# Softmax of one batch written over its scores in PSUM, and its constant added one column at a time

## The chip, the cores and the metric

One core of a Trainium2 chip runs the kernel. The engines are named as the profile names them: PE (TensorE matmuls), PEld (its weight loads), DVE (VectorE), ACT (ScalarE), POOL (GpSimd) and SP (SyncE, which issues DMAs). The metric is the device time of one execution in microseconds (us), lower is better. The kernel before takes 1260.88 us (median of three runs, 1260.35 to 1262.1).

## The reference

Attention over blocks of 64 positions, then a feed-forward layer with a piecewise activation, all in fp32:

```
q, k, v: (8 batches, 8 heads, 576 positions, 64)
scores = q k^T / 8, and -1e9 where key block > query block (blocks of 64)
attn   = exp(scores - rowmax); attn = attn / (rowsum(attn) + 1e-9)
x      = (attn v), heads side by side: (4608, 512)
h      = x @ w_in            (512 x 2048)
g      = h where h >= 1; 0 where h <= -1; (h + 1)^2 / 4 between
out    = g @ w_out           (2048 x 512)
```

## The kernel before

The work goes by **pairs** of heads: 8 batches of 4 pairs. `attention_steps` walks the pairs in eight steps each and starts parts of the next pair (loading, splitting, turning q and k) between the softmax steps of the current one. For a pair, each head's 576 x 576 scores are made in row tiles of 128 queries against only the keys that are not masked: group 0 is two tiles side by side in one PSUM bank (128 and 256 columns), group 1 is one tile of 384, group 2 one of 512 columns. The last 64 queries of both heads of the pair share one more tile of 576 columns, in two banks (`scores_last`).

For each group, `scores` does this: PE makes the scores in a PSUM bank `ps` (L483, L486); DVE takes the negated row maximum `nm` of each tile (L506); ACT writes the exponential into the SBUF tile `pr`, and its row sum into one column of `sm` (L510); DVE adds the constant 1e-9 to all the sums of the group (L492 in `inverse`: a 128 x 2 operation for group 0, 128 x 1 for the others), takes the reciprocal (L493), and multiplies `pr` in place by it, tile by tile (L516). Then PE turns `pr` with an identity (`turn`, L553 or L555) and multiplies it with v (`weighted`, L592).

Batches differ in their treatment. Batch 0 turns `pr` directly. From batch 1 on (`HOP`) `pr` first goes through a DMA into another buffer. From batch 2 on (`FAR`, `RAW`, and no longer `PLAIN`) all operands are split into a high and a low word, and the work of a pair is spread further; `add_words` (L614, L615) then adds the two halves of the product with v.

**Banks.** PSUM has eight banks here: one for the feed-forward's `ph`, four in the pool `ps_o`, three in `ps_w`. `work_bank` hands them out in turn; up to the 36th step it alternates between `ps_o` and `ps_w`, after that `ps_o` belongs to the feed-forward's output and attention has the three of `ps_w`. A bank can be written again once everything that read it is done: for a score bank in the kernel before, that is the exponential.

**The rest of the work.** `prepare_weights` turns the weights into split words during the first two batches: ACT and DVE work on each piece (L169 to L177), then POOL (L183, L187), for which the pieces stand in three buffers. From step 36 one feed-forward step goes with each attention step: `ffn_in` (L771: 12 matmuls), the activation (ACT L780, DVE L781, DVE L784, ACT L785), POOL's `gl` (L786), and `ffn_out` of the piece before (L795, L800). When attention ends, the remaining feed-forward runs alone.

**Order.** The order of the instructions on each engine is fixed when the program is built, by the framework's scheduler: it follows the order in the text as a priority and lets work go ahead that is ready earlier. Each engine then takes its instructions strictly in that order, and each waits for its operands by semaphores. A change of one operation can therefore move others.

Of the kernel before, what the change touches and what calls it, by code (L numbers as in the profile page):

```python
# [10 lines left out]
AF = mybir.ActivationFunctionType  # L11
ALU = mybir.AluOpType
# [11 lines left out]
def block_attn_then_ffn(  # L24
# [9 lines left out]
    nc = tc.nc  # L34
# [19 lines left out]
    EPS = 1e-9  # L54
# [4 lines left out]
    HOP = 1  # L59
    FAR = 2  # L60
    RAW = 2

    const = ctx.enter_context(tc.tile_pool(name="const", bufs=1))
    att1 = ctx.enter_context(tc.tile_pool(name="att1", bufs=1))
# [12 lines left out]
    def work_bank(name):  # L77

        banks["n"] += 1
        if banks["free"] and banks["n"] % 2:  # L80
            return ps_o.tile([P, 512], F32, tag="po", name=name)
        return ps_w.tile([P, 512], F32, tag="work", name=name)
# [23 lines left out]
    def last_blocks(t_):  # L106
# [19 lines left out]
        out=msel[:NTL, : NTL * BLK].rearrange("p (t c) -> p t c", c=BLK),  # L126
# [106 lines left out]
    def as_float32r(src, plain):  # L233

        if plain:
            wide = src.shape[1] > RING - 2 * S
            places = SPARE_WIDE if wide else SPARE
            moved = [places[spare[wide] % len(places)]]
            spare[wide] += 1
            if src.shape[1] > TCH:  # L240
                if "end" not in spare:
                    spare["end"] = att1.tile([P, G0 + P], F32R, tag="pa11", name="pre")[:, :BLK]
                moved.append(spare["end"])
            for i, dst in enumerate(moved):
                n = min(TCH, src.shape[1] - i * TCH)
                nc.sync.dma_start(dst[:, :n].bitcast(F32), src[:, i * TCH : i * TCH + n])
            return moved
        n, moved = src.shape[1], []
        wide = wide_tile(F32R, "prr")
        nc.sync.dma_start(wide[:, :n].bitcast(F32), src)  # L250
        for c0 in range(0, n, TCH):
            moved.append(wide[:, c0 : min(c0 + TCH, n)])
        return moved


    class Pair:
# [4 lines left out]
        def __init__(self, b, hp):  # L261
# [6 lines left out]
            self.hop = b >= HOP  # L268
            self.raw = b >= RAW

# [218 lines left out]

        def inverse(self, total):  # L490

            nc.vector.tensor_scalar_add(total, total, EPS)  # L492
            nc.vector.reciprocal(total, total)  # L493

        def scores(self, j, g):
            tiles = self.GROUPS[g]
            m = len(tiles)
            ps = work_bank("ps_s")
            pr = att3.tile([P, S], F32, tag="pr", name="pr")
            nm = small.tile([P, 2], F32, tag="nm", name="nm")  # L500
            sm = small.tile([P, 2], F32, tag="sm", name="sm")
            cols = [slice(at, at + (t + 1) * P) for t, at in tiles]
            for (t, _), cs in zip(tiles, cols):
                self.product(ps[:, cs], j, t * P, 0, (t + 1) * P, True, True)
            for i, cs in enumerate(cols):
                nc.vector.tensor_reduce(  # L506
                    out=nm[:, i : i + 1], in_=ps[:, cs], axis=AX.X, op=ALU.max, negate=True
                )
            for i, cs in enumerate(cols):
                nc.scalar.activation(  # L510
                    pr[:, cs], ps[:, cs], AF.Exp, bias=nm[:, i : i + 1], scale=1.0,
                    accum_out=sm[:, i : i + 1],
                )
            self.inverse(sm[:, :m])
            for i, cs in enumerate(cols):
                nc.vector.tensor_scalar_mul(pr[:, cs], pr[:, cs], sm[:, i : i + 1])  # L516
            self.pr[j, g] = as_float32r(pr[:, : cols[-1].stop], self.plain) if self.hop else [pr]

        def scores_last(self):

            half = S // 2
            pr = att3.tile([P, S], F32, tag="pr", name="pr")
            nm = small.tile([P, 3], F32, tag="nm", name="nm")
            sm = small.tile([P, 3], F32, tag="sm", name="sm")
            banks = []
            for i in range(2):
                ps = work_bank("ps_s")
                for j in range(2):
                    self.product(ps[:, :half], j, SM, i * half, half, j == 0, j == 1)
                nc.vector.tensor_reduce(  # L530
                    out=nm[:, i : i + 1], in_=ps[:, :half], axis=AX.X, op=ALU.max, negate=True
                )
                banks.append(ps)
            nc.vector.tensor_tensor(out=nm[:, 2:3], in0=nm[:, 0:1], in1=nm[:, 1:2], op=ALU.min)
            for i in range(2):
                nc.scalar.activation(
                    pr[:, i * half : (i + 1) * half], banks[i][:, :half], AF.Exp,
                    bias=nm[:, 2:3], scale=1.0, accum_out=sm[:, i : i + 1],
                )
            nc.vector.tensor_tensor(out=sm[:, 2:3], in0=sm[:, 0:1], in1=sm[:, 1:2], op=ALU.add)  # L540
            self.inverse(sm[:, 2:3])
            nc.vector.tensor_scalar_mul(pr, pr, sm[:, 2:3])
            self.pr["last"] = as_float32r(pr, self.plain) if self.hop else [pr]

# [341 lines left out]
```

## Time and profile before

| what | value |
|---|---|
| runs | 1260.88, 1262.1, 1260.35 us |
| span of the profiled execution | 1262.2 us (1.3 us above the median run) |
| busy over the span | PE 1193.1 us (95%), DVE 888.1 (70%), ACT 695.3 (55%), POOL 375.3 (30%) |
| attention of batch 0 ends (last L516) | at about 106 us |
| attention of batch 1 ends (last L516) | at about 257 us |
| attention of the last batch ends (last L516) | at about 1065 us |
| granted TensorE clock, mean | 0.986: 0.90 up to 107 us, 0.95 from there to 257 us, 1.00 up to 1100 us |

All times are from one profiled execution, counted from the start of its span. A busy PE is not a PE at its peak, because matmuls overlap and their ends are modelled; idle time of PE, on the other hand, is time in which nothing ran on it. For what a wait costs, the row to read is the one that names the engine that waited and what released it.

### The profile page before, as it was taken

How to read it: one execution, taken by the hardware profiler on the slowest of the kernel's cores; microseconds unless marked ns; L12 is line 12 of the kernel's file. 1: busy time of each engine (PE TensorE's matmuls, PEld its weight loads, DVE VectorE, ACT ScalarE, POOL GpSimd, SP SyncE). 2: the span in 40 equal slices, each digit the busy share in tenths (PEclk: the TensorE clock that was granted, in tenths of full speed). 3: DMA queues.
4: the chain of work that ended last, by engine and by line, in shares of the span. 5: the costliest groups of instructions: out<-in, count | busy, mean ns of one | idle time of the engine just before them, and what ended most of it. 6: DMA issues, size and time to landing. Idle time of an engine off the chain costs nothing.

```text
span 1262.2 us, 19823 instructions
## 1 busy us (share of the span) xinstructions
PE 1193.1 (95%) x6280; PEld 995.7 (79%) x6280; DVE 888.1 (70%) x2092; ACT 695.3 (55%) x1731; POOL 375.3 (30%) x366
## 2 busy tenths in 40 slices
PE   4887988999999999999999999999999999999998
PEld 3665876788888888888888888888888888888886
DVE  8888688658777877787777877787778776222322
ACT  5776666446565666565556565565656655222222
POOL 3444556312222222222222222222222222222222
PEclk9887999999999999999999999999999999999999
DMA  5566676778887654565555545554556433422432
GB/s 162 167 183 208 215 253 213 217 219 236 277 270 242 187 151 146 163 195 158 148 151 174 179 144 156 153 179 140 161 156 188 143 118 119 133 93 91 134 101 100
DMA packets 177191, 215.39 MB, mean 171 GB/s; under 512 B 109872, under 2 KB 128304, under 8 KB 176320
## 3 DMA queue, kind: packets, MB, share of 16 engines
q1 hardware_dynamic: 177088, 214.14, 55.3%
q8 instruction: 50, 0.82, 0.3%
q14 instruction: 53, 0.43, 0.1%
HBM read 134.74 MB, written 31.98 MB: 132 GB/s over the span
## 4 chain that ended last, share of the span: by engine, by line
PE 69%; DVE 17%; ACT 5%; issue 5%; DMA 3%; POOL 1%; SPq 0%; ACTq 0%; DVEq 0%; POOLq 0%
PE ph L771 27%; PE po L795 15%; PE po L800 8%; PE ps_av L592 8%; PE ps_s L483 4%; PE ps_s L486 3%; ACT pr L510 3%; PE ps_t L553 2%; DVE pr L516 2%; DVE t L781 2%; DVE pb L548 2%; DVE t L784 2%; ACT t L780 2%; DVE nm L506 2%; DVE sm L492 1%
## 5 line engine op out<-in xcount | busy, mean ns | idle before, releaser
L786 POOL TENSOR_TENSOR gl<-t,gh 128x512 fp32r<-128x512 f32 x144 | 186.1, 1292 | 530.9 <-ACT gh L785 360.6
L795 PE MATMUL po<-wo,gh 128*128 128x512 f32 x1152 | 295.2, 397 | 0.1
L795 PEld LDWEIGHTS po<-wo,gh 128*128 128x128 f32 x1152 | 211.9, 189 | 43.6 <-ACT gh L785 0.6
L771 PE MATMUL ph<-xh,wih 128*128 128x512 f32 x576 | 231.4, 402 | 4.7 <-DVE t L784 4.4
L771 PE MATMUL ph<-xh,wil 128*128 128x512 f32 x576 | 226.8, 394 | 0.0
L771 PE MATMUL ph<-xl,wih 128*128 128x512 f32 x576 | 226.1, 393 | 0.0
L781 DVE SCALAR_TENSOR_TENSOR t<-t 128x512 f32<-128x512 f32 x144 | 101.8, 707 | 162.6 <-ACT t L780 159.6
L510 ACT ACTIVATE pr<-ps_s,nm 128x128 f32<-128x128 f32 (+3 forms) x256 | 133.9, 526 | 83.8 <-DVE nm L506 81.2
L780 ACT ACTIVATE t<-ph 128x512 f32<-128x512 f32 x144 | 85.9, 597 | 158.1 <-PE ph L771 158.1
L785 ACT CAST gh<-t 128x512 fp32r<-128x512 f32 x144 | 89.5, 621 | 121.0 <-DVE t L784 120.7
L800 PE MATMUL po<-wo,gl 128*128 128x512 f32 x576 | 155.4, 392 | 0.0
L483 PE MATMUL ps_s<-ka,qa 68*128 68x288 f32 (+4 forms) x384 | 134.7, 366 | 16.6 <-ACT pr L510 7.8
L506 DVE TENSOR_REDUCE nm<-ps_s 128x1 f32<-128x128 f32 (+3 forms) x256 | 119.0, 483 | 13.8 <-PE ps_s L486 12.9
L771 PEld LDWEIGHTS ph<-xh,wih 128*128 128x128 f32 x576 | 108.9, 189 | 24.2 <-DVE t L784 4.7
L771 PEld LDWEIGHTS ph<-xh,wil 128*128 128x128 f32 x576 | 108.8, 189 | 23.6
L800 PEld LDWEIGHTS po<-wo,gl 128*128 128x128 f32 x576 | 108.6, 189 | 22.9
L380 POOL TENSOR_TENSOR vsr<-vn,vsr 128x256 fp32r<-128x256 f32 (+1 forms) x96 | 56.4, 588 | 233.0 <-ACT vsr L379 232.0
L771 PEld LDWEIGHTS ph<-xl,wih 128*128 128x128 f32 x576 | 109.2, 190 | 19.3
L516 DVE TENSOR_SCALAR pr<-pr,sm 128x128 f32<-128x128 f32 (+3 forms) x256 | 118.4, 486 | 6.1 <-DMA ka<-kb 0.3
L486 PE MATMUL ps_s<-kb,qb 128*128 128x288 f32 (+4 forms) x384 | 120.9, 322 | 0.0
L492 DVE TENSOR_SCALAR sm<-sm 128x1 f32<-128x1 f32 (+1 forms) x224 | 55.8, 249 | 77.1 <-ACT pr L510 74.4
L784 DVE TENSOR_TENSOR t<-ph,t 128x512 f32<-128x512 f32 x144 | 98.7, 686 | 2.1
(111 smaller groups left out, 1811.9 us busy)
## 6 DMA issues: line engine op xcount, KB each, us to landing
wo<-wo_split SPq DMA_DIRECT2D x144, 512.0 KB, 3.4
prr<-pr SPq DMA_DIRECT2D x96, 192.0 KB, 2.5
prr<-pr SPq DMA_DIRECT2D x48, 256.0 KB, 2.6
out_dram<-ob SPq DMA_DIRECT2D x36, 256.0 KB, 2.3
bits<-in_moe_w_in_dram SPq DMA_DIRECT2D x16, 512.0 KB, 4.6
bits<-in_moe_w_out_dram SPq DMA_DIRECT2D x16, 512.0 KB, 4.0
wo_split<-ws SPq DMA_DIRECT2D x16, 512.0 KB, 3.0
qa<-qb SPq DMA_DIRECT2D x63, 128.0 KB, 2.4
```

Of the source, the lines that this page charges most:

```text
L483: nc.tensor.matmul(ps, qa[:KA, j, c0 : c0 + P], ka[:KA, j, k0 : k0 + n], start=first, stop=False)
L486: nc.tensor.matmul(ps, qb[:, j, c0 : c0 + P], kb[:, j, k0 : k0 + n], start=False, stop=last)
L506: nc.vector.tensor_reduce(out=nm[:, i : i + 1], in_=ps[:, cs], axis=AX.X, op=ALU.max, negate=True)
L510: nc.scalar.activation(pr[:, cs], ps[:, cs], AF.Exp, bias=nm[:, i : i + 1], scale=1.0, accum_out=sm[:, i : i + 1],)
L516: nc.vector.tensor_scalar_mul(pr[:, cs], pr[:, cs], sm[:, i : i + 1])
L771: nc.tensor.matmul(ph, w[:, cc, fs], x[:, cc, xs], start=(cc == 0 and i == 0), stop=(cc == NCC - 1 and i == 2),)
L780: nc.scalar.activation(t_, ph, AF.Relu, bias=0.5, scale=0.5)
L781: nc.vector.scalar_tensor_tensor(out=t_, in0=t_, scalar=1.0, in1=t_, op0=ALU.min, op1=ALU.mult)
L784: nc.vector.tensor_tensor(out=t_, in0=ph, in1=t_, op=ALU.max)
L786: nc.gpsimd.tensor_tensor(out=gl, in0=t_, in1=gh.bitcast(F32), op=ALU.subtract)
L795: nc.tensor.matmul(po[tt], gh[:, ts_], wo[:, w, :], start=(fc == 0 and w == 0), stop=False)
L800: nc.tensor.matmul(po[tt], gl[:, ts_], wo[:, 0, :], start=False, stop=fc == NFC - 1)
```

## The change

Three edits in `Pair`:

- In `scores`, for batch 0 alone (`AT_HOME = 1`), the exponential is written over the scores in their own PSUM bank, and the multiplication by the reciprocal reads that bank and writes `pr` in SBUF. Batches 1 to 7 keep `pr` for both.
- In `inverse`, the constant is added in one instruction per column: two of 128 x 1 for group 0, where there was one of 128 x 2. The reciprocal stays one instruction for the group.
- In `scores_last`, for all batches, the addition of the two half sums and the addition of the constant become one instruction with two operations, with the second half sum as a per-partition scalar.

```
+    AT_HOME = 1
...
         def inverse(self, total):
-            nc.vector.tensor_scalar_add(total, total, EPS)
+            for i in range(total.shape[1]):
+                nc.vector.tensor_scalar_add(total[:, i : i + 1], total[:, i : i + 1], EPS)
             nc.vector.reciprocal(total, total)
...
+            raw = ps if self.b < AT_HOME else pr
             for i, cs in enumerate(cols):
                 nc.scalar.activation(
-                    pr[:, cs], ps[:, cs], AF.Exp, bias=nm[:, i : i + 1], scale=1.0,
+                    raw[:, cs], ps[:, cs], AF.Exp, bias=nm[:, i : i + 1], scale=1.0,
                     accum_out=sm[:, i : i + 1],
                 )
             self.inverse(sm[:, :m])
             for i, cs in enumerate(cols):
-                nc.vector.tensor_scalar_mul(pr[:, cs], pr[:, cs], sm[:, i : i + 1])
+                nc.vector.tensor_scalar_mul(pr[:, cs], raw[:, cs], sm[:, i : i + 1])
...
-            nc.vector.tensor_tensor(out=sm[:, 2:3], in0=sm[:, 0:1], in1=sm[:, 1:2], op=ALU.add)
-            self.inverse(sm[:, 2:3])
+            nc.vector.tensor_scalar(
+                out=sm[:, 2:3], in0=sm[:, 0:1], scalar1=sm[:, 1:2], scalar2=EPS,
+                op0=ALU.add, op1=ALU.add,
+            )
+            nc.vector.reciprocal(sm[:, 2:3], sm[:, 2:3])
```

In the changed kernel the lines below the edits count a few higher: L492 becomes L494, L493 L495, L506 L508, L516 L519, L615 L621.

From batch 2 on, PE's order is the same, and that of the other engines nearly so but for the edits themselves. DVE, in such a batch at group 0 of a pair's first head (`sm` are its row sums; `x` is the pair before's sum of two halves, after which a bank is free for PE); before:

```order
L506 TENSOR_REDUCE nm<-ps_s 128x1 x2
L615 TENSOR_TENSOR x_5004<-ps_av,xtmp 64x256
L492 TENSOR_SCALAR sm<-sm 128x2
L493 RECIPROCAL sm<-sm 128x2
L615 TENSOR_TENSOR x_5004<-ps_av,xtmp 64x256
L516 TENSOR_SCALAR pr<-pr,sm 128x128
L516 TENSOR_SCALAR pr<-pr,sm 128x256
```

and now:

```order
L508 TENSOR_REDUCE nm<-ps_s 128x1 x2
L621 TENSOR_TENSOR x_5018<-ps_av,xtmp 64x256
L494 TENSOR_SCALAR sm<-sm 128x1 x2
L495 RECIPROCAL sm<-sm 128x2
L621 TENSOR_TENSOR x_5018<-ps_av,xtmp 64x256
L519 TENSOR_SCALAR pr<-pr,sm 128x128
L519 TENSOR_SCALAR pr<-pr,sm 128x256
```

One row has become two of one column each; nothing else has moved.

In batches 0 and 1 the scheduler has also moved other work. DVE, from the first group 0 of the first pair (`qa`, `ka` are q and k turned, `bits` and `shifted` the weights); before:

```order
L174 TENSOR_SCALAR shifted<-bits 128x512
L458 CAST qa<-ps_qk 64x2x64
L492 TENSOR_SCALAR sm<-sm 128x2
L177 SCALAR_TENSOR_TENSOR bits<-bits,shifted 128x512
L493 RECIPROCAL sm<-sm 128x2
L492 TENSOR_SCALAR sm<-sm 128x1
L458 CAST ka<-ps_qk 64x2x64
L516 TENSOR_SCALAR pr<-pr,sm 128x128
L516 TENSOR_SCALAR pr<-pr,sm 128x256
```

and now:

```order
L175 TENSOR_SCALAR shifted<-bits 128x512
L494 TENSOR_SCALAR sm<-sm 128x1
L459 CAST qa<-ps_qk 64x2x64
L494 TENSOR_SCALAR sm<-sm 128x1
L178 SCALAR_TENSOR_TENSOR bits<-bits,shifted 128x512
L495 RECIPROCAL sm<-sm 128x2
L494 TENSOR_SCALAR sm<-sm 128x1
L459 CAST ka<-ps_qk 64x2x64
L519 TENSOR_SCALAR pr<-ps_s,sm 128x128
L519 TENSOR_SCALAR pr<-ps_s,sm 128x256
```

The first column's addition now stands ahead of `qa`, and the multiplications read `ps_s`, the score bank, instead of `pr`. A few dozen rows further the two orders differ in where a weight piece's three DVE operations stand: before, one piece's operations were spread between the row maxima of the second pair, and now they stand together ahead of them.

## The prediction

> **What bounds the kernel now.** I read the stages first, one row each: the attention of batch 0 (up to 107 us), of batch 1 (up to 257 us), of batches 2 to 7 (up to 1100 us). Columns: the stretch, its length, then busy time and count of PE, PEld, DVE, ACT and POOL, granted clock, DMA share, GB/s.
>
> ```profile
> 0.00:107.00 107.00, 74.64 (x385) 60.21 (x385) 91.68 (x240) 72.50 (x187) 41.88 (x45) 0.90 0.60 176
> 107.00:257.00 150.00, 133.78 (x668) 106.98 (x668) 116.50 (x254) 94.87 (x226) 75.57 (x63) 0.95 0.71 222
> 257.00:1100.00 843.00, 827.69 (x4542) 699.35 (x4541) 638.14 (x1539) 491.12 (x1259) 220.45 (x229) 1.00 0.57 174
> ```
>
> In batch 0 DVE is busy 91.7 of 107 us and PE idles for 32.4. In the long stretch PE is busy 827.7 of 843 us: it is what the stage waits for, and only its 15.3 us of idle time can be won there. So the next view is PE's waits in the long stretch: who waited, for whom, us in total, times, the longest.
>
> ```profile
> PE ps_s L483 <- ACT pr L510: 7.8, 24, 0.4
> PE ps_qk L443 <- DVE x L615: 6.9, 19, 0.4
> ```
>
> These two make 14.7 of the 15.3 us, about once each in every one of the 24 pairs. Both come from work on DVE, so I looked for DVE operations that take longer than their size explains. The groups of the long stretch (line, engine, operation, shapes, count, then busy us and mean ns, then idle time before them):
>
> ```profile
> L492 DVE TENSOR_SCALAR sm<-sm 128x2 f32<-128x2 f32 x48 | 26.0, 542 | 26.0 <-ACT pr L510 26.0
> L492 DVE TENSOR_SCALAR sm<-sm 128x1 f32<-128x1 f32 x120 | 18.4, 153 | 41.0 <-ACT pr L510 38.6
> L516 DVE TENSOR_SCALAR pr<-pr,sm 128x384 f32<-128x384 f32 x48 | 20.1, 419 | 1.7 <-DMA ka<-kb 0.3
> L516 DVE TENSOR_SCALAR pr<-pr,sm 128x256 f32<-128x256 f32 x48 | 16.7, 348 | 0.0
> L516 DVE TENSOR_SCALAR pr<-pr,sm 128x128 f32<-128x128 f32 x48 | 13.8, 286 | 1.6
> ```
>
> The same addition takes 542 ns on two columns and 153 ns on one. One element more cannot cost 389 ns; something holds the instruction. The order of time shows what.
>
> **Term A: the first head's group 0, batches 2 to 7.** One pair; columns: start us, us, engine, line, operation.
>
> ```profile
> 502.88 1.29 POOL L786 TENSOR_TENSOR gl<-t,gh 128x512 fp32r<-128x512 f32 x1 [0.98 <-ACT gh L785]
> 503.03 0.19 ACT L510 ACTIVATION_READ_ACCUMULATOR pr<-ps_s,nm 128x1 f32 x1
> ...
> 503.70 0.37 ACT L614 COPY xtmp<-ps_av 64x256 f32<-64x256 f32 x1
> 503.71 0.49 DVE L492 TENSOR_SCALAR sm<-sm 128x2 f32<-128x2 f32 x1 [0.77 <-ACT pr L510]
> ...
> 504.23 0.17 DVE L493 RECIPROCAL sm<-sm 128x2 f32<-128x2 f32 x1
> ...
> 504.43 0.43 DVE L615 TENSOR_TENSOR x<-ps_av,xtmp 64x256 f32<-64x256 f32 x1
> ...
> 505.00 0.25 PE L443 MATMUL ps_qk<-ident_r,qk 128*128 128x128 f32 x1 [0.38 <-DVE x L615]
> ```
>
> The two-column addition starts at 503.71 and ends at 504.20, when POOL's gl ends (502.88 + 1.29 = 504.17). The reciprocal and x follow without a gap, and PE, which idled for 0.38 us, starts once x is done. So this is the wait on POOL, handed on to PE. The one-column form shows no such wait on average. In the changed kernel the first column's addition fits into the 0.77 us in which DVE idled, since its sum is there at 503.22; the second takes 0.15 us from 503.71. The reciprocal then ends near 504.07. Now x has another condition, ACT's copy, which ends at 503.70 + 0.37 = 504.07: x can start at 504.10 in place of 504.43. That is 0.33 us earlier, and PE has 0.38 us of idle time to give up. Over the 19 waits of the row: 19 x 0.33 = **6.3 us**. Bounds: nothing, if PE's next operand comes late anyway, and the row's 6.9.
>
> **Term B: the second head's group 0, same batches.**
>
> ```profile
> 519.95 1.29 POOL L786 TENSOR_TENSOR gl<-t,gh 128x512 fp32r<-128x512 f32 x1 [5.78 <-issue]
> ...
> 520.68 0.58 DVE L492 TENSOR_SCALAR sm<-sm 128x2 f32<-128x2 f32 x1 [0.27 <-ACT pr L510]
> ...
> 521.30 0.17 DVE L493 RECIPROCAL sm<-sm 128x2 f32<-128x2 f32 x1
> ...
> 521.50 0.55 DVE L516 TENSOR_SCALAR pr<-pr,sm 128x128 f32<-128x128 f32 x2
> ...
> 523.42 0.55 DVE L506 TENSOR_REDUCE nm<-ps_s 128x1 f32<-128x384 f32 x1
> ...
> 524.00 0.58 ACT L510 ACTIVATE pr<-ps_s,nm 128x384 f32<-128x384 f32 x1 [2.14 <-DVE nm L506]
> ...
> 524.72 0.50 PE L483 MATMUL ps_s<-ka,qa 68*128 68x512 f32 x1 [0.29 <-ACT pr L510]
> ```
>
> Again the addition ends with POOL's gl (519.95 + 1.29 = 521.24, against 521.26). From there DVE works without a pause up to the row maximum at 523.42, ACT's exponential waits for that, and PE waits 0.29 us for the exponential to free a bank. Here part of the gain is handed back: the addition would end at 520.83, the reciprocal at 521.03, and the multiplication, which works from SBUF to SBUF on many columns, stands before the same POOL operation until 521.24. It starts near 521.27 in place of 521.50: 0.23 us of the 0.43 remain. 24 x 0.23 = **5.5 us**; bounds nothing and the row's 7.8. A and B together: 11.8 us, between 0 and 14.7.
>
> **Term C: batch 0's multiplications.** All of them up to 107 us, the sum of the two halves in `scores_last`, and the row maxima, the nearest rows for an operation that reads one operand from PSUM:
>
> ```profile
> L516 DVE TENSOR_SCALAR pr<-pr,sm 128x384 f32<-128x384 f32 x8 | 7.7, 961 | 0.1
> L516 DVE TENSOR_SCALAR pr<-pr,sm 128x128 f32<-128x128 f32 x8 | 6.8, 850 | 0.0
> L516 DVE TENSOR_SCALAR pr<-pr,sm 128x256 f32<-128x256 f32 x8 | 6.2, 773 | 0.0
> L506 DVE TENSOR_REDUCE nm<-ps_s 128x1 f32<-128x512 f32 x8 | 5.5, 687 | 1.8 <-PE ps_s L486 1.7
> L506 DVE TENSOR_REDUCE nm<-ps_s 128x1 f32<-128x384 f32 x8 | 4.4, 548 | 0.0
> L516 DVE TENSOR_SCALAR pr<-pr,sm 128x512 f32<-128x512 f32 x8 | 3.9, 482 | 0.1
> L506 DVE TENSOR_REDUCE nm<-ps_s 128x1 f32<-128x256 f32 x8 | 3.3, 413 | 0.0
> ...
> L540 DVE TENSOR_TENSOR sm<-sm 128x1 f32<-128x1 f32 x4 | 2.4, 607 | 0.0
> L506 DVE TENSOR_REDUCE nm<-ps_s 128x1 f32<-128x128 f32 x8 | 2.3, 284 | 1.6 <-PE ps_s L486 1.6
> ```
>
> The multiplications take 7.7 + 6.8 + 6.2 + 3.9 = 24.6 us. Unhindered they would take 8 x (286 + 348 + 419 + 482 ns) = 12.3, by the long stretch's rows and this 512 row; the other 12.3 are waiting. One place shows on whom:
>
> ```profile
> 63.44 0.36 ACT L510 ACTIVATE pr<-ps_s,nm 128x128 f32<-128x128 f32 x1
> ...
> 65.62 1.40 POOL L365 TENSOR_TENSOR ks<-kn,ks 128x576 fp32r<-128x576 f32 x1 [0.25 <-DVE sm L493]
> 65.73 2.12 DVE L516 TENSOR_SCALAR pr<-pr,sm 128x128 f32<-128x128 f32 x2
> ...
> 66.97 0.66 POOL L315 MEMSET vs<- 128x320 f32 x2
> ...
> 68.48 0.42 DVE L171 TENSOR_SCALAR bits<-bits 128x512 f32<-128x512 f32 x1
> ```
>
> Two multiplications that need 0.63 us last 2.12, through POOL's ks (to 67.02) and its MEMSETs (to 67.63). Read from PSUM, I price them like the row maxima, which stay at one duration throughout: 8 x (284 + 413 + 548 + 687) = 15.5 us. So the price of reading PSUM is 3.2 us, the waits saved 12.3, net 9.1 on DVE. The fused sum saves another 4 x 607 = 2.4 us: the one instruction that stays costs what the L492 row shows for one column. Direct sum: 11.5 us.
>
> [...]
>
> How much of 11.5 is on the path? The chain of work that ended last, up to 107 us, by line:
>
> ```profile
> by line: DVE pr L516 12.0%; issue 11.3%; PE ps_av L592 11.0%; PE ps_t L555 6.6%; DVE nm L506 4.6%; DMA ka<-mrow 4.2%; PE ps_qk L423 3.2%; DVE bits L171 3.2%; DVE bits L177 2.9%; DMA qn<-in_q_dram 2.7%; DVE shifted L174 2.7%; PE ps_s L483 2.
> ```
>
> 12.0% of 107 is 12.8 us of the multiplications' 24.6: half. And part of a saved wait is handed on, as in term B, to the next such operation on DVE. In the place above the two multiplications would end 1.42 us earlier (0.70 in place of 2.12), but L171, which now starts at 68.48, would then meet the MEMSETs and be held to about 67.65: 0.83 of 1.42 are kept, 0.6. That leaves 11.5 x 0.5 x 0.6 = 3.5, say 4 us. Against it stands the bank: it is now held until the multiplication has read it, some 2 us longer, and PE gets its next bank later. ACT writes its exponential into PSUM, which no row shows; I take its present duration. For the bank I set 2 us: one or two of the 24 score groups of batch 0 in PE's way. Term C: **2 us** gained. Bounds: 11.5 gained, if nothing is handed on and all is on the path; 10 lost, if nothing is gained on the path and the banks of a third of the 24 score groups come 1.3 us late.
>
> **Term D: batch 1** keeps `pr` in SBUF and has only the additions:
>
> ```profile
> L492 DVE TENSOR_SCALAR sm<-sm 128x2 f32<-128x2 f32 x8 | 3.4, 427 | 5.5 <-ACT pr L510 5.5
> ```
>
> 8 x (427 - 153) = 2.2 us on DVE; half of it kept: **1 us**, between 0 and 2.2. The fused sum in `scores_last` of batches 1 to 7 takes one addition of 0.15 us off DVE per pair where PE has no wait in the rows above: nothing. The 64 additional one-column operations (64 x 0.153 = 9.8 us of DVE time) lie in DVE's idle time before the second sum, as in A and B. Without that idle time each would cost 0.15.
>
> **Sum.** 11.8 + 2 + 1 = 14.8 us off the profiled execution's 1262.2: 1247.4. That execution is 1.3 us above the median of the runs, so I forecast **1246 us**. What is won early stays won: after 257 us PE never has long to wait.
>
> **Rivals.**
> 1. *The wait stays with POOL.* What holds the two-column addition holds the next many-column operation as long. Then B gives nothing and C only its loss; A remains, since x follows there and not a multiplication: 1260.9 - 6.3 - 1 = about 1253. For it: in B half is already handed on by my own count. Against: in A nothing of that kind stands behind, and B's POOL operation has only 0.2 us left.
> 2. *Batch 0 gives its full share.* DVE is the fullest engine there, and waits off the chain count too once the chain is shorter: A, B and D plus 10 us, 1260.9 - 12.8 - 10 = about 1238. For it: DVE at 91.7 of 107 us. Against: PE and "issue" hold as much of the chain.
> 3. *No change.* PE's two waits are only its modelled ends; a DMA that brings `pr` back ends next, and the time stays: 1260. Against: the long stretch shows no wait of PE for a DMA.
> 4. *Slower: the banks of batch 0.* Exponential and multiplication lie far apart: in the rows of term C the one of 128 columns ends at 63.80, and its pair of multiplications at 67.85. With 24 score groups in seven banks, PE cannot begin the scores two or three groups on. If 16 of them (groups 0 and 1) delay PE by 2 us each, batch 0 grows by 32: 1260.9 + 32 - 12.8 = 1280. It decides from about 0.8 us per group (12.8 / 16). Against: PE's order has the turning of a group, which needs the multiplication anyway, close behind the reuse of its bank.
>
> **How the numbers follow.** Forecast 48% (its own range 1240 to 1251), rival 1 17%, rival 2 17%, rival 3 7%, rival 4 11%. The predicted time is the forecast's. The range 1233 to 1257 takes in rivals 1 and 2 with the bounds of C on the side of gain, and leaves out rivals 3 and 4. A measurement of this kernel can tell about 0.2% (2.5 us) from no change: faster 82%, same 7%, slower 11%.
>
> **What would show it.** A and B: the two-column group of L492 is gone, all additions near 153 ns; PE's waits for x fall from 6.9 to about 1 us and those for the exponential from 7.8 to about 2, and the long stretch is some 12 us shorter. B's handing on: the 128-column multiplication there lasts about 0.5 us. C: the four rows at 284 to 687 ns, the L171 and L174 rows longer than before, batch 0 ending 0 to 5 us earlier. It is wrong if PE's waits in batches 2 to 7 stay at 15 us in sum, or if PE waits in batch 0 for multiplications before it makes scores.

## The result and the profile after

The changed kernel takes 1245.48 us (median of four runs, 1241.76 to 1247.91); the kernel before, timed beside it on the same chip, 1261.49 (1260.35 to 1268.99). The ratio is 0.9854, with a 95% interval of 0.9822 to 0.9886. The forecast was 1246.0.

The profiled execution has a span of 1242.2 us against 1262.2, a difference of 20.0. The medians differ by only 16.0. A run's time is about 1.8 us longer than its span (1243.98 against 1242.2 for this execution), so the profiled execution after is 1.5 us below its median, and the one before, at about 1264.0, some 2.5 us above 1261.49. The 1.3 us given for it ahead of the prediction set a span against a run's time. I take a stage to end where the last 128x512 multiplication by the reciprocal in its batch ends:

| stage | before, us | after, us | difference | forecast |
|---|---|---|---|---|
| batch 0 | 106.9 | 104.1 | -2.8 | -2 (C) |
| batch 1 | 150.5 | 150.8 | +0.3 | -1 (D) |
| batches 2 to 7 | 808.0 | 790.6 | -17.4 | -11.8 (A and B) |
| the rest | 196.8 | 196.8 | 0 | 0 |

So the signs of A and B together and of C came as forecast, that of D did not, and the term of the long stretch was half as large again as forecast. The stage rows of that stretch, cut to those ends, in the columns of the prediction (stretch, length, busy time and count of PE, PEld, DVE, ACT, POOL, granted clock, DMA share, GB/s); first before:

```profile
257.40:1065.40 808.00, 792.69 (x4376) 670.18 (x4376) 625.50 (x1518) 480.17 (x1239) 212.61 (x223) 1.00 0.58 176
```

and after:

```profile
254.80:1045.40 790.60, 789.18 (x4377) 670.16 (x4376) 610.73 (x1543) 480.53 (x1236) 212.29 (x221) 1.00 0.58 178
```

PE idled for 15.3 us and now idles for 1.4. That explains 13.9 of the 17.4. The other 3.5 are PE's busy time, with the same number of matmuls; more on them below. Both waits of PE of the prediction are gone: PE's waits from 240 to 1090 us after are the one row

```profile
PE ps_t L559 <- DMA vsr<-pr: 0.9, 1, 0.9
```

The chain of work that ended last, as shares of the whole span by engine, points the same way. Before:

```profile
PE 69%; DVE 17%; ACT 5%; issue 5%; DMA 3%; POOL 1%; SPq 0%; ACTq 0%; DVEq 0%; POOLq 0%
```

and after:

```profile
PE 79%; DVE 2%; DMA 1%; ACT 1%; issue 0%; POOL 0%; ACTq 0%
```

The two rows can't be compared as they stand: the shares after add up to 83%, because that chain could be followed back only to 200 us, and so lacks batch 0 and most of batch 1. Summed over batches 2 to 7 alone, where both chains are whole, PE's share went from 73.6% to 97.4%, DVE's from 15.1% to 1.3% and ACT's from 6.5% to 0.8%.

The groups on DVE in that stretch after the change (count, then busy us and mean ns, then idle time before them):

```profile
L494 DVE TENSOR_SCALAR sm<-sm 128x1 f32<-128x1 f32 x192 | 29.4, 153 | 58.1 <-ACT pr L513 54.8
...
L519 DVE TENSOR_SCALAR pr<-pr,sm 128x128 f32<-128x128 f32 x48 | 14.0, 292 | 1.9 <-DVE sm L495 0.3
...
L543 DVE TENSOR_SCALAR sm<-sm 128x1 f32<-128x1 f32 x24 | 5.1, 214 | 27.4 <-ACT pr L539 27.4
```

All additions of the constant take 153 ns. The 128-column multiplication, which I expected at about 0.5 us in the second head's group 0, stays at 292 ns on average over both heads (286 before): 47 of the 48 took 285 to 290 ns, and one, which started 0.46 us before gl's end, 542. In the others nothing was handed on. The order of time shows why. First the place of term A after the change (start us, us, engine, line, operation):

```profile
494.81 1.29 POOL L792 TENSOR_TENSOR gl<-t,gh 128x512 fp32r<-128x512 f32 x1 [0.99 <-ACT gh L791]
...
495.18 0.15 DVE L494 TENSOR_SCALAR sm<-sm 128x1 f32<-128x1 f32 x1 [0.32 <-ACT pr L513]
...
495.64 0.15 DVE L494 TENSOR_SCALAR sm<-sm 128x1 f32<-128x1 f32 x1 [0.30 <-ACT pr L513]
...
495.82 0.17 DVE L495 RECIPROCAL sm<-sm 128x2 f32<-128x2 f32 x1
...
496.02 0.43 DVE L621 TENSOR_TENSOR x<-ps_av,xtmp 64x256 f32<-64x256 f32 x1
...
496.60 0.25 PE L444 MATMUL ps_qk<-ident_r,qk 128*128 128x128 f32 x1
```

Both additions run in 0.15 us while POOL's gl, from 494.81 to 496.10, is under way. The sum x starts 0.08 us before gl ends, where it started 0.26 after it: 0.34 us earlier, as forecast (0.33). PE's matmul no longer has a wait in front of it. Then the place of term B:

```profile
478.85 1.28 POOL L792 TENSOR_TENSOR gl<-t,gh 128x512 fp32r<-128x512 f32 x1 [5.79 <-issue]
...
479.34 0.39 DVE L494 TENSOR_SCALAR sm<-sm 128x1 f32<-128x1 f32 x2
...
479.76 0.17 DVE L495 RECIPROCAL sm<-sm 128x2 f32<-128x2 f32 x1
...
479.97 0.55 DVE L519 TENSOR_SCALAR pr<-pr,sm 128x128 f32<-128x128 f32 x2
...
481.88 0.55 DVE L508 TENSOR_REDUCE nm<-ps_s 128x1 f32<-128x384 f32 x1
...
483.19 0.50 PE L484 MATMUL ps_s<-ka,qa 68*128 68x512 f32 x1
```

The two multiplications start at 479.97, while gl runs until 480.13, and still take the 0.55 us that they took before. The row maximum starts 1.75 us after gl's end, where it started 2.18 after it: the whole 0.43 us are kept.

In batch 0 (up to 107 us) the multiplications read the bank:

```profile
L519 DVE TENSOR_SCALAR pr<-ps_s,sm 128x512 f32<-128x512 f32 x8 | 6.0, 745 | 0.1
...
L519 DVE TENSOR_SCALAR pr<-ps_s,sm 128x384 f32<-128x384 f32 x8 | 4.9, 609 | 0.1
...
L519 DVE TENSOR_SCALAR pr<-ps_s,sm 128x256 f32<-128x256 f32 x8 | 3.8, 473 | 0.0
...
L519 DVE TENSOR_SCALAR pr<-ps_s,sm 128x128 f32<-128x128 f32 x8 | 2.7, 344 | 0.1
```

That is 17.4 us, against 24.6 before and 15.5 forecast. Part of what they no longer wait falls on the weight pieces' first operation, L171 before and L172 after, both up to 107 us; before:

```profile
L171 DVE TENSOR_SCALAR bits<-bits 128x512 f32<-128x512 f32 x14 | 7.0, 498 | 2.6 <-ACT bits L169 2.1 <-issue 0.6
```

and after:

```profile
L172 DVE TENSOR_SCALAR bits<-bits 128x512 f32<-128x512 f32 x15 | 10.6, 703 | 4.9 <-ACT bits L170 4.9
```

Each takes 205 ns longer on average, 3.1 us over 15.

### The profile page after: what moved, and what is told of

The parts are those of the page before. It is cut to its first block, busy times and chain, and to the rows that moved or that the text cites. A ratio compares the mean times of both kernels' runs of the same rounds, so it can differ in the third digit from the quotient of the medians.

```text
span 1242.2 us, 19834 instructions
## 1 busy us (share of the span) xinstructions
PE 1186.9 (96%) x6280; PEld 994.7 (80%) x6280; DVE 861.5 (69%) x2124; ACT 698.2 (56%) x1731; POOL 375.2 (30%) x366
## 4 chain that ended last, share of the span: by engine, by line
PE 79%; DVE 2%; DMA 1%; ACT 1%; issue 0%; POOL 0%; ACTq 0%
PE ph L777 29%; PE po L801 19%; PE po L806 10%; PE ps_av L598 8%; PE ps_s L484 5%; PE ps_s L487 4%; PE ps_t L559 3%; PE ps_qk L403 1%; PE ps_qk L444 0%; DMA vsr<-pr 0%; ACT pr L513 0%; DVE nm L508 0%; DVE t L787 0%; DVE bits L178 0%; DVE t L790 0%
## 5 line engine op out<-in xcount | busy, mean ns | idle before, releaser
L513 ACT ACTIVATE pr<-ps_s,nm 128x128 f32<-128x128 f32 x224 | 117.2, 526 | 66.2 <-DVE nm L508 63.1
L508 DVE TENSOR_REDUCE nm<-ps_s 128x1 f32<-128x128 f32 (+3 forms) x256 | 119.1, 483 | 16.2 <-PE ps_s L487 15.4
L777 PEld LDWEIGHTS ph<-xh,wil 128*128 128x128 f32 x576 | 108.4, 188 | 23.5
L381 POOL TENSOR_TENSOR vsr<-vn,vsr 64x64 fp32r<-64x64 f32 (+1 forms) x96 | 56.7, 591 | 225.0 <-ACT vsr L380 225.0
L519 DVE TENSOR_SCALAR pr<-pr,sm 128x128 f32<-128x128 f32 x224 | 95.3, 446 | 5.8 <-DVE sm L495 0.5
L559 PEld LDWEIGHTS ps_t<-ident_r,prr 128*128 128x128 f32 x600 | 68.6, 139 | 22.1
```

Of the source, the lines that this page charges most:

```text
L508: nc.vector.tensor_reduce(out=nm[:, i : i + 1], in_=ps[:, cs], axis=AX.X, op=ALU.max, negate=True)
L513: nc.scalar.activation(raw[:, cs], ps[:, cs], AF.Exp, bias=nm[:, i : i + 1], scale=1.0, accum_out=sm[:, i : i + 1],)
L559: nc.tensor.transpose(out.bitcast(F32R), src, ident_r)
L777: nc.tensor.matmul(ph, w[:, cc, fs], x[:, cc, xs], start=(cc == 0 and i == 0), stop=(cc == NCC - 1 and i == 2),)
```

## The experiments

All ratios are to the kernel before, timed in the same job. In the three jobs its medians were 1263.99, 1263.12 and 1262.56 us.

**The parts, one at a time.** The additions column by column, and nothing else:

```
-            nc.vector.tensor_scalar_add(total, total, EPS)
+            for i in range(total.shape[1]):
+                nc.vector.tensor_scalar_add(total[:, i : i + 1], total[:, i : i + 1], EPS)
```

> Only the addition column by column. Theory POOL (the two-column addition stands still until a POOL instruction ends, the one-column form does not, and PE waits for what follows it in batches 2 to 7): nearly all of the gain, some 16 to 18 us, ratio about 0.987; PE's two waits (7.8 and 6.9 us) fall under 2 us. Rival HOME (the gain is that of batch 0's banks): under 3 us.

Measured: 1250.32 us, ratio 0.9894 [0.9861, 0.9927]. Batches 2 to 7 took 791.1 us, 16.9 less than before: this edit alone makes the term of the long stretch. PE's waits in that stretch are down to one of 0.3 us. The 13.7 us in all are less than the 16 to 18 expected. In the profile batch 0 ended 2.3 us later than in the kernel before, while the edit lets DVE's additions go sooner; PE's and DVE's orders differ there from those before, and that this is the cause is not shown.

Batch 0 at home in PSUM, and nothing else:

```
+    AT_HOME = 1
...
+            raw = ps if self.b < AT_HOME else pr
...
-                    pr[:, cs], ps[:, cs], AF.Exp, bias=nm[:, i : i + 1], scale=1.0,
+                    raw[:, cs], ps[:, cs], AF.Exp, bias=nm[:, i : i + 1], scale=1.0,
...
-                nc.vector.tensor_scalar_mul(pr[:, cs], pr[:, cs], sm[:, i : i + 1])
+                nc.vector.tensor_scalar_mul(pr[:, cs], raw[:, cs], sm[:, i : i + 1])
```

> Only batch 0's exponential in its bank and the multiplication from there. Theory POOL: 2 to 4 us, all before 107 us; the long stretch keeps PE's two waits of about 15 us in sum. Rival HOME: 13 us or more. Rival BANKS (the bank held longer costs as much as the waits saved): no gain or slower.

Measured: 1264.91 us, 1.0009 [0.9990, 1.0029]: no difference. The 2 to 4 us expected did not come. In the profile batch 0 is 2.0 us shorter and batch 1, where no bank is held longer, 2.0 us longer. The two waits of PE in batches 2 to 7 stand as before (from 275 to 1050 us):

```profile
PE ps_s L484 <- ACT pr L512: 7.4, 23, 0.4
PE ps_qk L444 <- DVE x L617: 7.2, 19, 0.7
```

The fused sum of the last tile, and nothing else:

```
-            nc.vector.tensor_tensor(out=sm[:, 2:3], in0=sm[:, 0:1], in1=sm[:, 1:2], op=ALU.add)
-            self.inverse(sm[:, 2:3])
+            nc.vector.tensor_scalar(
+                out=sm[:, 2:3], in0=sm[:, 0:1], scalar1=sm[:, 1:2], scalar2=EPS,
+                op0=ALU.add, op1=ALU.add,
+            )
+            nc.vector.reciprocal(sm[:, 2:3], sm[:, 2:3])
```

> Only the two sums and the constant in one instruction in scores_last. Theory POOL: within 2 us of the kernel before; the one place with a price is batch 0, where the sum of two SBUF operands took 607 ns (1.8 us in all). A gain of more than 4 us would say that this edit was undervalued.

Measured: 1266.86 us, 1.0021 [1.0005, 1.0038]: 2.9 us slower, where within 2 us was expected. Batches 2 to 7 took 808.4 us (808.0 before), so there it is worth nothing, as forecast. In the profile the loss is in batch 1, which took 155.4 instead of 150.5 us; batch 0 was 2.2 us shorter.

**The parts do not add up.** In medians split gives 13.7, home -0.9 and fuse -2.9, together 9.9; the whole change gave 16.0 in its first comparison and 18.5 in a later one (all_three, below). In batches 2 to 7 the parts do add up (16.9, 0.2 and -0.4 against 17.4). What does not is batches 0 and 1, where each edit gave another order of the instructions. PE's order in batches 2 to 7 is the same in all of these kernels.

**What holds the addition.** The theory was that an operation of DVE from SBUF to SBUF on more than one column has to wait for POOL's operation to end. A narrower form was that only an even number of columns is held. To tell them apart, group 0's addition was made over three columns (the added lines, shortened):

```
+            sm = small.tile([P, 4], ...)
+            if m == 2:
+                nc.vector.memset(sm[:, 2:3], 1.0)
+            wide = sm[:, :3] if m == 2 else sm[:, :1]
+            nc.vector.tensor_scalar_add(wide, wide, EPS)
+            nc.vector.reciprocal(sm[:, :m], sm[:, :m])
```

> The kernel before, with the addition of group 0 in one instruction over three columns (the third is set to 1.0 beforehand and not used). Theory POOL in its narrow form (only an even number of columns goes two at a time, and only that form stands still for POOL): about 155 ns each and the same gain as the split, 15 to 18 us less the 64 small settings. Rival WAIT (the long duration is the wait for the second sum, or belongs to any addition over more than one column): some 540 ns as before, and no gain.

Measured: 1266.52 us, 1.0031 [1.0012, 1.0049]. The addition is held as ever, and so is PE; the group in batches 2 to 7 (257 to 1050 us) and the waits (275 to 1050 us):

```profile
L517 DVE TENSOR_SCALAR sm<-sm 128x3 f32<-128x3 f32 x47 | 25.3, 539 | 25.1 <-ACT pr L512 25.1
```

```profile
PE ps_s L483 <- ACT pr L512: 7.6, 23, 0.4
PE ps_qk L443 <- DVE x L619: 7.1, 21, 0.4
```

So the narrow form fell; of the forms of this addition tried, only one column is free (153 ns, against 542 on two columns and 539 on three). What sets one column apart from more is not shown by any run here; only that the instruction is held.

That it is POOL, and POOL's gl, was tested by taking gl away. The low word of the activation is left out, and its matmuls read the high word a second time:

```
-        gl = ffn.tile([P, TCH], F32R, tag="gl", name="gl")
...
-        nc.gpsimd.tensor_tensor(out=gl, in0=t_, in1=gh.bitcast(F32), op=ALU.subtract)
...
-        return gh, gl, wo
+        return gh, gh, wo
```

> The kernel before with the two-column addition, but without POOL's gl (L786): the low word of the activation is left out, and the matmuls that would read it read the high word again, so that PE's work stays the same. Theory POOL (gl is what the addition stands still for): the two-column additions of batches 2 to 7 take about 155 ns, PE's two waits go, and the time falls by 15 to 20 us although the addition was not split. Rival WAIT: 540 ns stay, no gain.

Measured: 1243.69 us, 0.9850 [0.9828, 0.9872]. The two-column addition, unchanged in the code, is now short:

```profile
L492 DVE TENSOR_SCALAR sm<-sm 128x2 f32<-128x2 f32 x48 | 8.1, 169 | 25.7 <-ACT pr L510 25.7
```

16 ns above the one-column form, and batches 2 to 7 take 788.8 us, 1.8 less than after the change. PE's two waits are gone too. The holder is gl. The rival that needs no POOL for the hold, and for which the 540 ns of three columns would do as well, falls with this: of what comes before the addition on DVE and ACT nothing was changed.

**The price of the bank.** After the multiplications of batch 0, in the kernel before, one more small operation reads the bank and so keeps it as long as the change would:

```
+            if self.b < 1:
+                nc.vector.tensor_copy(nm[:, :1], ps[:, cols[-1].stop - 1 : cols[-1].stop])
```

> The kernel before, and in batch 0 one more DVE copy of one score column behind each multiplication, which keeps the bank until then without any of the edits. 24 copies of at most 0.2 us are 5 us of DVE, half of it on the path. My step (2 us for the banks): 2 to 5 us slower in all. Rival BANKS (2 us for 16 groups): 20 us or more slower.

Measured: 1268.85 us, 1.0045 [1.0032, 1.0057], 5.7 us slower, a little more than the 2 to 5 expected. Rival 4's 32 us for batch 0 is far off. But the profile has only 0.3 us of the loss in batch 0 and 4.6 in batch 1, where the bank is not held and the order is another: the bank's price in batch 0 is not isolated by this run.

Where every batch keeps its exponential at home, the bank does get in the way:

```
-    AT_HOME = 1
+    AT_HOME = 8
```

> The changed kernel with all batches at home in their banks. From batch 2 on attention has three banks, not seven, and POOL hinders the multiplications there by only 0.13 us on 512 columns. Theory (what a bank held longer costs depends on how many banks there are): PE waits for banks several times per pair, 1 to 3 us per pair in 24 pairs, so 25 to 70 us slower than the changed kernel. Rival: PE has the feed-forward to fill it, and the time stays within 10 us.

Measured: 1263.59 us, 1.0000 [0.9986, 1.0015]; the gain of the change is gone. Batches 2 to 7 took 814.1 us, 23.5 more than with one batch at home, about 1 us per pair. In all the loss is some 18 us by the two ratios, less than the 25 expected at least. PE's waits from 240 to 1090 us, and the multiplication they wait for (257 to 1050 us):

```profile
PE ps_qk L444 <- DVE pr L519: 12.5, 23, 0.6
PE ps_av L598 <- DVE kb L397: 1.4, 5, 0.3
```

```profile
L519 DVE TENSOR_SCALAR pr<-ps_s,sm 128x512 f32<-128x512 f32 x47 | 35.3, 751 | 1.6
```

This is rival 4's mechanism, in the batches where attention has three banks: PE cannot turn the next pair's q and k until the multiplication has read its bank. These waits explain about 13.6 of the 23.5 us, the growth of PE's idle time in batches 2 to 7 (1.4 to 15.0 us). The other 9.9 us are in PE's busy time (789.2 to 799.0 us with the same number of matmuls). PE's order is another one there, so that the whole of the 23.5 is not shown to be the bank's price.

**Two batches at home.** With `AT_HOME = 2` instead:

> The changed kernel with batch 1 too at home in its banks. In batch 1 the multiplications wait some 6 us for POOL and would pay about 3 us more for reading PSUM: between 3 us faster and 3 us slower than the changed kernel, that is 1242 to 1249 us; no clear difference.

Measured: 1239.07 us, 0.9813 [0.9791, 0.9835], below the range that was expected. A second time, in the next job, beside the changed kernel again:

> The changed kernel with batches 0 and 1 at home. If the 6 us of the first comparison (1239 against 1245, on different days of the chip) are real: 1237 to 1241 us, 4 to 8 us faster than all_three, all between the end of batch 0 and that of batch 1. If they were scatter of the first two stages: within 2 us of all_three.

> The changed kernel once more, as the mark for the other three on the same chip: 1242 to 1248 us, ratio about 0.985.

Measured: home2_again 1240.66 us, 0.9827 [0.9808, 0.9846]; the changed kernel 1244.09, 0.9854 [0.9832, 0.9875]. Two batches at home are 3.4 us faster in that job, between the two forecasts, with intervals that overlap: likely, not shown. Both of its medians are below both of the changed kernel's (1245.48 and 1244.09). Its profiles show 145.5 and 147.9 us for batch 1, against 150.8 and 150.7 for the changed kernel. They also show how much one profile can tell of these stages: the same kernel reached the end of batch 1 at 249.6 us in one job and at 253.1 in the other.

**Is the fused sum a loss?** The changed kernel with the old sum in `scores_last`, at one batch and at two batches at home:

```
-            nc.vector.tensor_scalar(
-                out=sm[:, 2:3], in0=sm[:, 0:1], scalar1=sm[:, 1:2], scalar2=EPS,
-                op0=ALU.add, op1=ALU.add,
-            )
-            nc.vector.reciprocal(sm[:, 2:3], sm[:, 2:3])
+            nc.vector.tensor_tensor(out=sm[:, 2:3], in0=sm[:, 0:1], in1=sm[:, 1:2], op=ALU.add)
+            self.inverse(sm[:, 2:3])
```

> The changed kernel with scores_last as before (the two sums added first, then the constant). Theory FUSE COSTS (the fused instruction alone lost 2.9 us, so it loses here too): 2 to 4 us faster than all_three. Rival ORDER (the edits of the first two stages do not add up, because each gives the scheduler another order there; the fused form itself is worth nothing or a little): from the same to 4 us slower than all_three.

> Batches 0 and 1 at home, column by column, scores_last as before. Theory FUSE COSTS: 2 to 4 us faster than home2_again, 1235 to 1238. Rival ORDER: anything from 3 faster to 5 slower, by the first two stages alone; batches 2 to 7 take 790 us in either case.

Measured: 1242.43 us, 0.9842 [0.9821, 0.9863], with one batch at home: 1.7 us faster without the fused sum, less than can be told, and in neither forecast's range. With two: 1245.84, 0.9869 [0.9847, 0.9890]: 5.2 us slower without it, against FUSE COSTS and just past ORDER's 5. The same edit lost 2.9 us alone and gained 5.2 here, depending on what else is in the program. So its own cost is not the cause; batches 2 to 7, where it stands 24 times, took 790.2 and 789.7 us without it and 791.3 and 790.0 with it. What moves is batches 0 and 1: with two batches at home they ended at 253.1 us with the fused sum and at 257.8 without. The order of the instructions differs there between these kernels; that it is the cause is argued from this, and which rows of the order cost it was not settled: PE's waits of batch 1 differ in each of these kernels.

## Why the prediction was right, and where it was not

The forecast's time was right to 0.5 us, but that closeness is partly luck: 14.8 us were forecast, 16.0 measured in the medians (18.5 in a later job) and 20.0 in the profiles. In the profiles A and B gave 5.6 us more than forecast, C 0.8 more and D 1.3 less. The 16.0 us of the medians are less than A and B alone gave in the profiles, though C and D were to add 3.

**Terms A and B, mis-sized: 11.8 forecast, 17.4 measured** (split_only: 16.9). The mechanism is as told: POOL's gl holds the two-column addition (542 ns, and 169 in no_gl), one column is free (153 ns; three are held too, at 539 in three_columns). Two steps made the size wrong.

- "The multiplication ... stands before the same POOL operation until 521.24" was wrong. It started 0.16 us before gl's end and lost nothing, so the 0.2 us per pair that I had handed on stayed gained. Both rows of waits went whole, 14.7 us where I counted 11.8 (2.3 more in B, 0.6 in A); with the other idle time PE's fell by 13.9 us, 2.1 more than I counted.
- The upper bound was wrong in kind. I took PE's idle time (14.7 us in the two waits) as all that could be won. The gain was 17.4, since PE's busy time fell too, by 3.5 us with the same number of matmuls. The durations of its matmuls sum to the same before and after (1494.1 and 1493.8 us); the busy time counts overlapping matmuls once. So the matmuls overlap more when no wait comes between them: 3.5 us over the 43 waits is about 0.08 us for each, beside its idle time. The other runs agree. In those that keep both waits (home_only, fuse_only, three_columns, hold_only) PE was busy for 792.7 to 793.2 us in batches 2 to 7; in the seven without them (home8 apart) for 787.5 to 789.7. That it is the wait itself that costs the overlap is my reading, and no run isolates it.

**Term C: 2 forecast, 2.8 measured**, but this does not prove its steps. The waits are gone from the multiplications, as forecast, and about half of the 7.2 us gained on DVE was handed on to the weight pieces, where 0.4 was forecast (L171 to L172, 498 to 703 ns; L174 to L175, 483 to 529). The price of reading PSUM was too low: each of the four rows is 58 to 61 ns above the row maximum of its size (344, 473, 609, 745 against 284, 413, 548, 687). The row maximum has no per-partition scalar; the fused sum, which has one, takes 61 ns more than the addition that hasn't (214 against 153). That the scalar is the reason is not shown. And edits that leave batch 0's multiplications as they are move its end by 2 us either way (split_only +2.3, fuse_only -2.2). Home_only, which is C without the fused sum, gave 2.0 us there in the profile and nothing in the median. So a 2.8 us gain there does not show C.

**Term D: 1 forecast, -0.3 measured**. Batch 1 lies between 145.5 and 156.6 us in the kernels above, and a term of 1 us cannot be seen there.

**The fused sum** was priced at 153 ns and takes 214. Worth nothing in batches 2 to 7 was right (808.4 against 808.0).

**The rivals.** 1, the wait that stays with POOL, fell with the 292 ns of the multiplication. (Its sum left out the loss of C that it speaks of; with 2 us for it the time is about 1256, still far off.) 2, batch 0's full share of 10 us: batch 0 gave 2.8. 3, no change, fell: no wait for a DMA took the place, but one of 0.9 us. 4, the banks: in batch 0 PE's only waits for multiplications after the change are in front of turning, not in front of making scores. The row in PE's waits up to 104 us, before:

```profile
PE ps_t L555 <- DVE pr L516: 4.5, 7, 0.9
```

and after:

```profile
PE ps_t L561 <- DVE pr L519: 9.2, 6, 2.8
```

The turning needs these multiplications anyway. The mechanism itself is real, and shows where there are three banks (12.5 us of PE's time in 23 waits in home8).

## What to carry to other kernels

Where a tiny DVE operation on a statistic takes much longer than its size explains, look at what POOL is doing when it ends: here, doing two columns in two instructions of one column made both free, at 0.15 us each in idle time, for 1.1% of the kernel's time (split_only). Put a PE wait's price a little above its idle time, and do not take the idle time for the ceiling: here 13.9 us less of it came with 17.4 us. And when an edit makes the scheduler write another order, compare the stages one by one: here the 5.2 us between two variants that differ in the last tile's sum came from batches 0 and 1 alone (4.7 us in their profiles), though that sum stands in all eight.

## What was not expected of the hardware

**A held operation lost 0.2 us less than the hold.** Two 128x512 multiplications of the kernel before; the first starts with all of gl ahead of it, the second with 0.19 us left:

```profile
294.55 1.28 POOL L786 TENSOR_TENSOR gl<-t,gh 128x512 fp32r<-128x512 f32 x1 [8.51 <-ACT gh L785]
...
294.59 1.52 DVE L516 TENSOR_SCALAR pr<-pr,sm 128x512 f32<-128x512 f32 x1
...
309.50 1.29 POOL L786 TENSOR_TENSOR gl<-t,gh 128x512 fp32r<-128x512 f32 x1 [0.60 <-ACT vsr L379]
...
310.60 0.49 DVE L516 TENSOR_SCALAR pr<-pr,sm 128x512 f32<-128x512 f32 x1
```

The first ends 0.28 us after gl (295.83 to 296.11), though it takes 0.49 unhindered. The second ends 0.30 after gl and takes the unhindered time. So 0.2 us of the operation pass beside POOL's operation as the profile records it. Either its first 0.2 us are not held, or POOL lets go a little before its recorded end; no run tells which. These 0.2 us are why the handing-on of term B did not happen: the first of its multiplications started 0.16 us before gl's end and took its 286 ns.

**Reading PSUM, the multiplication wasn't held at all.** In batch 0 after the change, three multiplications (128, 256 and 384 columns) beside POOL's operation from 41.92 to 43.35 us take 1.25 us together:

```profile
41.92 1.43 POOL L188 TENSOR_TENSOR ws<-bits,ws 128x512 fp32r<-128x512 f32 x1 [3.50 <-ACT ws L186]
...
42.11 1.25 DVE L519 TENSOR_SCALAR pr<-ps_s,sm 128x128 f32<-128x128 f32 x3
```

None of the 32 that read PSUM in batch 0 is long: the eight of each size lie within 20 ns of one another (331 to 351 ns at 128 columns, 735 to 752 at 512), though 16 of the 32 lie wholly inside a POOL operation. The slope is about twice that from SBUF: (745 - 344) / 384 = 1.04 ns per column, against (482 - 286) / 384 = 0.51.

**ACT's exponential was a little shorter into PSUM than into SBUF.** The exponential of batch 0 up to 107 us before, into SBUF:

```profile
L510 ACT ACTIVATE pr<-ps_s,nm 128x512 f32<-128x512 f32 x8 | 5.5, 689 | 5.2 <-DVE nm L506 5.2
...
L510 ACT ACTIVATE pr<-ps_s,nm 128x128 f32<-128x128 f32 x8 | 3.0, 376 | 1.2 <-DVE nm L506 1.2
```

and up to 104 us after, into PSUM:

```profile
L513 ACT ACTIVATE ps_s<-ps_s,nm 128x512 f32<-128x512 f32 x8 | 5.3, 664 | 5.1 <-DVE nm L508 5.1
...
L513 ACT ACTIVATE ps_s<-ps_s,nm 128x128 f32<-128x128 f32 x8 | 2.7, 342 | 0.4 <-DVE nm L508 0.3
```

25 and 34 ns shorter. I had taken the duration into SBUF.
